# Six weight slots, 56 score blocks, small passes on GpSimd: a new plan for a fused attention and MLP kernel

## The chip, the cores and the metric

The kernel runs on one core of a Trainium2 chip. The metric is the device time of one execution in microseconds (us); the kernel before takes 736.29 us, the median of three runs that lie between 736.22 and 736.51. The engines are called as the profile calls them: PE is TensorE (matmul), PEld its weight loads, DVE is VectorE, ACT is ScalarE, POOL is GpSimd, SP is SyncE, which here only issues DMAs. PSUM has eight banks; a bank holds one block of 128 x 512 fp32.

## What is computed

```
x: 2048 x 512, 32 heads of 16                        # bf16 everywhere
g = sigmoid((x * gate_w).sum(-1))
q, k, v = split(x @ wqkv)
a = (softmax(q k^T / 4) v) @ wo                      # attention
h = gelu(layernorm(x) @ w1)                          # mixer MLP
x1 = x + shift(h) @ w2                               # four quarters, moved by 1, -1, 2, -2 rows
b = x1 + gelu(layernorm(x1) @ w3) @ w4               # w3: 512 x 1792, w4: 1792 x 512
out = g * a + (1 - g) * b
```

## The kernel before

**Scores.** There are 32 rounds (4 chunks of 512 queries, 4 groups of 8 heads, and the even or the odd heads of a group). A round has 64 score tiles: 16 blocks of 128 keys for each of 4 heads, which sit in four 32-row strips of PE. That makes 2048 tiles of 128 x 512. The q of a round is stored with the other four heads set to zero: that is what the two masks mE and mO do (L1209 to 1212). A QK matmul (L1482) writes a tile to a bank, and one of two engines turns it into exp(score). ACT takes two or three banks in one instruction (L1577). DVE instead makes bf16 bits by a linear map (L1609, "p1"), and then three more copies of the block with a constant added to the bits (L1652 on DVE, L1654 on POOL); the four together approximate the exponential. So a tile of ACT needs one PV matmul and a tile of DVE four (L1707). `close_pair` decides which of the three added copies of a pair go to DVE and which to POOL, by the numbers GP2 and GP3.

**Score blocks.** The exp values of a tile wait for their PV matmuls in one of NPROB = 40 blocks of `prob` (L887, L934). A pair of DVE tiles that has begun holds one of NTOK = 3 tokens until its last copy is made.

**The rest.** Projections, the MLP and the output projection are matmuls in column strips (`gen`, L1105 to 1131), each followed by an evacuation of its bank on DVE. Layernorm (`normalise`, L1290) makes rs on POOL and nm on DVE, then 32 passes over 128 x 512 on DVE (L1304); each result is written to DRAM (L1308) and read back transposed (L1314). The passes of L1366 multiply x1 by 1 - g. The three Gelu blocks run on ACT (L1324).

**Weights.** NW = 9 slots of 4 KB a partition hold the transposed x chunks, wk, wv, w1, w2, w3 and w4; each of w3 and w4 is loaded once. `wo` has a tile of its own (L901).

**The order.** Nothing is scheduled on the chip. A model of the engines in the kernel's own code (`Sim`) runs at build time: it takes jobs by priority, by when their inputs are ready and by free slots, and writes down the order of every queue, which the engines then follow with semaphores. Its choices are steered by some 30 numbers (`BASE`, L524) which `STEPS` (L548 to 881) changes every eight tiles. Other work enters by the count of score tiles done: `P_W1`, `P_W3`, `P_LD` and the like (L504 to 520). A POOL instruction and a DVE pass with `port=True` are never planned at once, and the POOL one gets a dependency on the last such DVE pass (`in_port_order`, L319).

**The start.** x chunk 0 comes by two plain DMAs, one from SP and one from the ACT queue (L1029), is transposed by 16 PE matmuls against an identity (L1143), copied out by ACT and DVE (L1155), and projected in column strips into kT and q (`k_first`, L1161; L1200, L1202). Chunks 2 and 3 are read by transposing DMAs (L1038), four each, all from SP.

**The end.** Behind the last PV matmul DVE forms the denominators of the last round (L2082 to 2085) and the last oT (L2092); PE adds the known part of the output (L2060), and four blocks are evacuated (L2099, L2101) and stored by four DMAs (L2103).

Of the kernel before, what the change touches and what calls it, by code (L numbers as in the profile page):

```python
# [470 lines left out]
def kernel(  # L471
# [48 lines left out]
    P_LD = (450, 888)  # L520
# [28 lines left out]
        0: dict(S_PRIO=0.3, GP2=1, DVE_STOP_L=7, SL0=0, IDLE_NS=864, BRES=2, AHEAD=16, AT_SH=69, HOLE=3, CAP3=5,  # L549
            AFIRST=1, AGE=20000),  # L550
        1: dict(DVE_STOP=2, URG=3, GATE=3, E_PRIO=0.1),
        2: dict(MAXU=4),
        3: dict(P1_PRIO=0.743, SL1=130, BRES=0, PV_IDLE=0.117, HOLE=2, RES=1),
        4: dict(P1_PRIO=0.414, GP2=0, DVE_STOP=6, URG=5, SL1=60, IDLE_NS=374, AHEAD2=24, PV_IDLE=0.731, MAXU=9, ROT=3,
            HOLE=7, MAXG=2, CAP3=0, RES=0, E_PRIO=2),
        5: dict(GP3=0.633, PV_FULL=0.947, LIMD=2, AGE=12000, JOIN=2),
        6: dict(URG=11, SL0=60),
        7: dict(GP2=0.655, GP3=0.967, DVE_STOP=13, URG=5, AHEAD2=13, PV_FULL=0.916, PRESS=15, MAXG=1, LIMD=3, AFIRST=0,
            AGE=20000, ROWM=3, LIMA=4, JOIN=0),
        8: dict(P1_PRIO=0.136, GP2=1, DVE_STOP=6, URG=2, DVE_ALONE=-81, SL0=0, B_LOW=5, AHEAD2=16, PRESS=18, MAXU=7,  # L560
            ROT=2, GATE=2, E_PRIO=0.25, AFIRST=1, ROWM=99, LIMA=3, JOIN=1),
# [12 lines left out]
        19: dict(SL0=130, AHEAD2=32, AFIRST=0),
        20: dict(S_PRIO=0.38, GP2=1, DVE_STOP=6, DVE_STOP_L=16, URG=5, EARLY=99, SL0=0, B_LOW=8, PV_FULL=0.813,
            PV_IDLE=0.117, PRESS=26, MAXU=7, ROT=3, AT_SH=69, HOLE=7, E_PRIO=0.25, AFIRST=1),
        21: dict(B_LOW=2, PRESS=22, MAXU=3, AT_SH=0, CAP2=5, LIMD=3),
        22: dict(URG=11, DVE_WAIT=4, DUE_SH=0),
        23: dict(URG=5, B_LOW=8, DVE_WAIT=3, PV_FULL=0.86, PRESS=26, DUE_SH=-14, AT_SH=69, CAP2=6, CAP3=4, LIMD=4),
        24: dict(IDLE_NS=459, AFIRST=2),  # L580
        25: dict(P1_PRIO=0.414, S_PRIO=0.178, DVE_STOP=13, IDLE_NS=864, B_LOW=5, AHEAD2=24, PV_FULL=0.97, PV_IDLE=0.731,
            PRESS=11, MAXU=2, ROT=0, DUE_SH=0, MAXG=3, AFIRST=1, ROWM=3),
        26: dict(S_PRIO=0.5),
        27: dict(S_PRIO=0.178, GP3=1, DVE_STOP=8, SL1=0, IDLE_NS=537, PV_FULL=1, PV_IDLE=0.117, PRESS=18, ROT=2,
            DUE_SH=16, MAXG=1, AFIRST=0),
# [417 lines left out]
    def W(name):  # L1003
        return wb[name].slot
# [1128 lines left out]
```

## Time and profile before

| | before |
|---|---|
| median of three runs | 736.29 us |
| the profiled execution | 735.27 us |
| its span, first to last instruction | 733.3 us |
| granted TensorE clock | 0.999 |
| busy: PE, DVE, ACT, POOL | 723.8, 698.6, 720.0, 452.7 us |
| DMA | 34.60 MB, mean 47 GB/s |

The profiled execution is the one from which all durations come; 2.0 us of its time lie outside the span. In a row of a group, the numbers behind the bar are the busy time of the group, the mean duration of one instruction in ns, and how long its engine stood idle just before such instructions, with what ended that. Two neighbours on an engine overlap in the trace, so the step from one start to the next is shorter than the duration. The ends of matmuls are modelled, so PE looks busy while it holds a finished result.

### The profile page before, as it was taken

The numbers are of one execution on the slowest core, as the hardware profiler recorded it, in microseconds if no ns is written. First come the engines' busy times: TensorE is split into PE (matmuls) and PEld (weight loads), VectorE is DVE, ScalarE is ACT, GpSimd is POOL, SyncE is SP. The second block draws the span as 40 slices with busy tenths as digits, with TensorE's granted clock in tenths as the row PEclk, the third lists the DMA queues.
The fourth block names the chain that finished last, engine by engine and source line by source line (L and its number), as shares of the span: only waits on it lengthen the run. The fifth ranks groups of instructions, "written<-read, shape, count | busy, mean of one in ns | idle before, by whom it ended". The sixth has DMA issues, their size and how long they took to land.

```text
span 733.3 us, 23826 instructions
## 1 busy us (share of the span) xinstructions
PE 723.8 (99%) x9517; PEld 212.3 (29%) x9518; DVE 698.6 (95%) x1493; ACT 720.0 (98%) x751; POOL 452.7 (62%) x452
## 2 busy tenths in 40 slices
PE   9999999999999999999999999999999999999997
PEld 5434322222222222222322222222222232222222
DVE  6999999999999999999999999999999999999997
ACT  7999999999999999999999999999999999999995
POOL 3456685778867666658545555566576765575442
PEclk9999999999999999999999999999999999999999
DMA  8504223111212033024100100001100010000001
GB/s 189 162 19 77 80 66 71 28 45 57 72 49 53 21 96 69 21 81 96 32 25 10 46 28 21 27 23 43 27 20 18 7 32 24 28 26 19 14 22 41
DMA packets 67094, 34.60 MB, mean 47 GB/s; under 512 B 46748, under 2 KB 62380, under 8 KB 66984
## 3 DMA queue, kind: packets, MB, share of 16 engines
q1 hardware_dynamic: 66040, 32.56, 17.7%
q8 instruction: 74, 1.21, 0.7%
q10 hardware_dynamic: 944, 0.52, 0.2%
q14 instruction: 36, 0.29, 0.2%
HBM read 17.40 MB, written 6.81 MB: 33 GB/s over the span
## 4 chain that ended last, share of the span: by engine, by line
PE 64%; ACT 11%; DVE 4%; issue 2%; POOL 0%; ACTq 0%; DVEq 0%
PE banks L1707 24%; PE banks L1482 22%; PE banks L1112 17%; ACT prob L1577 6%; ACT hT L1324 2%; ACT hB L1324 2%; DVE prob L1609 1%; DVE prob L1652 1%; ACT L1324 1%; DVE x_sb L1357 0%; ACT L1326 0%; DVE st L1284 0%; DVE w L1415 0%; POOL prob L1654 0%; PE banks L2060 0%
## 5 line engine op out<-in xcount | busy, mean ns | idle before, releaser
L1577 ACT ACTIVATE prob<-banks 128x1024 bf16<-128x1024 f32 (+1 forms) x728 | 675.5, 1102 | 1.1 <-PE banks L1482 0.2
L1654 POOL TENSOR_SCALAR prob<-prob 128x1024 uint16<-128x1024 uint16 x390 | 400.3, 1045 | 233.4 <-DVE prob L1652 110.9
L1609 DVE TENSOR_SCALAR prob<-banks 128x512 uint16<-128x512 f32 x577 | 380.3, 684 | 17.4 <-PE banks L1482 12.9
L1707 PE MATMUL banks<-prob,V 128*17 128x512 bf16 (+1 forms) x3785 | 321.6, 381 | 0.2
L1482 PE MATMUL banks<-q,kT 32*128 32x512 bf16 x2048 | 280.1, 384 | 1.5 <-ACT prob L1577 0.7
L1652 DVE TENSOR_SCALAR prob<-prob 128x1024 uint16<-128x1024 uint16 x480 | 179.5, 422 | 2.0 <-PE banks L1707 0.6
L1482 PEld LDWEIGHTS <-kT 32*128 32x128 bf16 x2048 | 70.0, 90 | 295.3 <-ACT prob L1577 269.2
L1707 PEld LDWEIGHTS <-V 128*17 128x17 bf16 (+1 forms) x3785 | 71.8, 88 | 116.7 <-issue 94.9
L1112 PE MATMUL banks<-xnT,w 128*32 128x512 bf16 x1152 | 89.4, 383 | 0.0
L1112 PE MATMUL banks<-w,hT 128*32 128x512 bf16 x688 | 64.5, 384 | 0.0
L1746 POOL TENSOR_TENSOR oT<-accsb,bcs 128x512 bf16<-128x512 f32 x31 | 39.5, 1273 | 26.7 <-DVE prob L1652 21.5
L1112 PEld LDWEIGHTS <-w 128*32 128x32 bf16 x1936 | 41.0, 95 | 48.9 <-issue 27.0
L1112 PE MATMUL banks<-w,w 128*32 128x256 bf16 (+1 forms) x784 | 41.5, 308 | 0.4 <-DVE prob L1609 0.4
L1112 PE MATMUL banks<-w,hB 128*32 128x512 bf16 x448 | 36.0, 382 | 0.6 <-ACT hB L1324 0.6
L1123 PE MATMUL banks<-wo,oD 32*128 32x512 bf16 x64 | 24.6, 384 | 0.0
L1112 PEld LDWEIGHTS <-hT 128*32 128x32 bf16 x688 | 15.9, 95 | 20.5 <-issue 15.1
L1284 DVE BATCH_NORM_STATS2 st<-x_sb 128x6 f32<-128x512 bf16 x32 | 21.5, 678 | 0.0
L1728 DVE COPY accsb<-banks 128x512 f32<-128x512 f32 x31 | 21.1, 680 | 0.2 <-PE banks L1707 0.2
L1112 PE MATMUL banks<-wo,oD 128*32 128x512 bf16 x176 | 21.0, 384 | 0.0
L1112 PE MATMUL banks<-w,wq 128*32 128x512 bf16 x256 | 19.4, 382 | 1.0 <-DVE accsb L1728 1.0
L1378 DVE CAST hB<-banks 128x512 bf16<-128x512 f32 x28 | 19.0, 682 | 0.9 <-PE banks L1112 0.9
L1324 ACT ACTIVATE hT<-hT 128x7168 bf16<-128x7168 bf16 (+1 forms) x3 | 19.4, 6452 | 0.0
(94 smaller groups left out, 246.8 us busy)
## 6 DMA issues: line engine op xcount, KB each, us to landing
bcs<-rr SPq DMA_DIRECT2D x124, 64.0 KB
xn_dram<-xn SPq DMA_DIRECT2D x32, 128.0 KB
w<-in_B_w_dram SPq DMA_DIRECT2D x5, 512.0 KB
oD<-oT SPq DMA_DIRECT2D x124, 16.0 KB
w<-in_B_w_dram SPq DMA_DIRECT2D x4, 448.0 KB
out_dram<-ot SPq DMA_DIRECT2D x14, 128.0 KB
x_sb<-in_A_x_dram SPq DMA_DIRECT2D x3, 512.0 KB
w<-in_A_wqkv_dram SPq DMA_DIRECT2D x2, 256.0 KB
```

What stands on the lines that cost most here:

```text
L1112: units.append([Op("col", j, lambda j=j, lf=lf, rf=rf, n0=n0, n1=n1, st=st, sp=sp: nc.tensor.matmul(get()[32 * j:32 * j + 32, n0:n1], lhsT ...
L1123: o = Op("row", i, lambda: nc.tensor.matmul(get(), lhsT=lf(0, P)[rows], rhs=rf()[rows], start=False, stop=True, tile_position=(32 * i, 0), ...
L1284: a = dve(600, deps, lambda: nc.vector.bn_stats(out=sb.slot[:], in_=x_sb[:, t, :]), prio=6, at=at, acq=[sb])
L1324: g = nc.scalar.activation(out=ap, in_=ap, func=ACT.Gelu_apprx_tanh)
L1482: o = Op("row", i, lambda: nc.tensor.matmul(dst(), lhsT=kT[G][32 * i:32 * i + 32, kt * P:(kt + 1) * P], rhs=qbuf[G, c].slot[32 * i:32 * i ...
L1577: job = act(hold, ops, lambda: nc.scalar.activation(out=prob[:, pb.cut(), :].bitcast(BF16), in_=unit()[:, rb.cut(), :], func=ACT.Exp, scal ...
L1609: return nc.vector.tensor_scalar(out=prob[:, b0.cut() if w == 2 else b0.bufs[h0].slot, :], in0=unit()[:, rb.cut() if w == 2 else rb.bufs[0 ...
L1652: return nc.vector.tensor_scalar(out=cut(k), in0=cut(0), scalar1=float(SHIFT * k), scalar2=None, op0=ALU.add)
L1654: return nc.gpsimd.tensor_scalar(out=cut(k), in0=cut(0 if both else 2), scalar1=1.0, scalar2=float(SHIFT * (k if both else 1)), op0=ALU.mu ...
L1707: return nc.tensor.matmul(one(accs[r])[32 * i:32 * i + n, :], lhsT=lhs(n), rhs=rhs(), start=st and not edge, stop=True, tile_position=(0, ...
L1728: e = dve(PSUM_NS, round_ops[r], lambda: nc.vector.tensor_copy(out=ab.slot[:], in_=one(accs[r])), acq=[ab], prio=0, frees=[accs[r], Call(a ...
L1746: n = gp(1250, d3, lambda: nc.gpsimd.tensor_tensor(out=ob.slot[:], in0=ab.slot[:], in1=bb.slot[:], op=ALU.mult), acq=[ob], frees=[ab, bb], ...
```

## The change

1. NPROB goes from 40 to 56, NTOK from 3 to 5, NW from 9 to 6. `wo` moves into one of the six slots. w3 and w4 are loaded twice, once for each pair of chunks, so eight more loads are issued; w2 and wo are loaded later (tile 330 and 855). The windows of w1 and of the second half of w3 begin later.
2. 76 passes of 128 x 512 go from DVE to POOL: 30 masks of q, 32 of layernorm, 14 products with 1 - g.
3. Chunk 0 of x is no longer loaded and transposed by PE: four transposing DMAs read it, slices 0 and 2 from SP, 1 and 3 from ACT. Twelve full-array matmuls (`first`) make q and kT of it; ACT and DVE evacuate half of q each. x_sb of chunk 0 is loaded later, for the layernorm alone.
4. At the end the first two output blocks leave in one DMA, all known parts come behind the last PV, and y of the last chunk lies in the slots of `xnT`.
5. A few durations in the model change, and `STEPS` is replaced throughout.

```diff
-    P_W1 = (143, 440)
+    P_W1 = (195, 445)
-    P_W3 = ((610, 710), (710, 840), (1200, 1390), (1400, 1570))
+    P_W3 = ((610, 710), (710, 840), (1245, 1400), (1410, 1570))
-    P_LD = (450, 888)
+    P_LD = ((450, 1190), (845, 1575))
...
-    NPROB, NTOK, NW = 40, 3, 9
+    NPROB, NTOK, NW = 56, 5, 6
...
-    xa, xb = (start(e, 3000.0, lambda q, a=a: q.dma_start(out=x_sb[:, a:a + 2, :], in_=x_src(0, a, a + 2)))
-              for e, a in (("SP", 0), ("ACT", 2)))
+    def xT_dma(c, part, k):
+        return lambda q: q.dma_start(out=W(f"x{c}{part}")[:, k, :], in_=x_by_d[c * 512:(c + 1) * 512, k], transpose=True)
     dl_w["q0"] = start("SP", 2600.0, col(wq, 0, 128))
     dl_w["k0"] = start("ACT", 2900.0, col(W("k"), D, D + 128))
+    for k in range(KT):
+        j_xT[0, 0, k] = start(("SP", "ACT")[k % 2], 2000.0, xT_dma(0, 0, k), 1800.0 if k < 2 else 1300.0)
+    j_x1 = [start("SP", 2600.0, lambda q: q.dma_start(out=x_sb[:, 4:8, :], in_=x_src(1, 0, 4)))]
...
+    def first(t):
+        qb = qbuf[0, 0] = Buf("q", 128)
+        bq, ba, bb = (Buf("bank", 1) for _ in range(3))
...
+        def mm():
+            for k in range(KT):
+                for b, w, n0, n1 in ((bq, wq, 0, 512), (ba, W("k"), 0, 256), (bb, W("k"), 256, 512)):
+                    guard(b, nc.tensor.matmul(one(b)[:, 0:n1 - n0], lhsT=w[:, k, 0:P], rhs=W("x00")[:, k, n0:n1], start=k == 0,
+                                              stop=k == KT - 1, skip_group_check=True))
+        def evacuate():
+            nc.scalar.activation(out=qb.slot[:, 0, 0:256], in_=one(bq)[:, 0:256], func=ACT.Copy, scale=mE[:])
+            nc.vector.tensor_scalar(out=qb.slot[:, 0, 256:512], in0=one(bq)[:, 256:512], scalar1=mE[:], scalar2=None,
+                                    op0=ALU.mult)
+            sim.readers[ba] = [nc.scalar.copy(out=kT[0][:, 0:256], in_=one(ba)[:, 0:256])]
...
         for p, m in ((0, mE), (1, mO)):
-            j_q[G, c, p] = dve(262, [e, j_m3] + ([j_q[G, c, 0]] if p else []), lambda p=p, m=m: nc.vector.tensor_scalar(
-                out=qb.slot[:, p, :], in0=qf.slot[:], scalar1=m[:], scalar2=None, op0=ALU.mult), prio=0.3, port=True,
+            j_q[G, c, p] = gp(600, [e, j_m3] + ([j_q[G, c, 0]] if p else []), lambda p=p, m=m: nc.gpsimd.tensor_scalar(
+                out=qb.slot[:, p, :], in0=qf.slot[:], scalar1=m[:], scalar2=0.0, op0=ALU.mult, op1=ALU.add), prio=0.3,
...
-            g = dve(323, [m], lambda t=t, xb=xb: nc.vector.tensor_scalar(
+            g = gp(600, [m], lambda t=t, xb=xb: nc.gpsimd.tensor_scalar(
                 out=xb.slot[:], in0=x_sb[:, t, :], scalar1=rs[which][:, t:t + 1], scalar2=nm[which][:, t:t + 1],
...
-            jx1g[t] = dve(262, [last[t % 4], jgate], lambda t=t: nc.vector.tensor_scalar(
+            jx1g[t] = gp(600, [last[t % 4], jgate], lambda t=t: nc.gpsimd.tensor_scalar(
...
-                    ybuf[tt // 2] = Buf("w", 10 ** 6)
+                    ybuf[tt // 2] = Buf("xnT", 10 ** 6)
...
-    for k in range(KT):
-        x_transposes(0, (k,), j_x0)
-    k_first()
-    q_proj(0, 0, -1)
+    first(6200.0)
...
-    for cs in PAIRS:
+    for cs, at3, at4 in zip(PAIRS, *P_LD):
+        for i in range(KT):
+            wload(f"3{i}", B_w3[i * P:(i + 1) * P, :], 2 * FT)
+            dl_w[f"3{i}"].prio, dl_w[f"3{i}"].at = 6, at3 + 10 * i
+        for i in range(4):
+            wload(f"4{i}", B_w4[512 * i:min(F, 512 * (i + 1)), :], 8)
+            dl_w[f"4{i}"].prio, dl_w[f"4{i}"].at = 7, at4 + 10 * i
         mlp2(cs, s2, at_of, gate_job)
...
     for tt in (1, 3):
-        add_y(tt, tt not in early)
-    for tt in range(4):
-        if tt not in early:
-            known(tt, range(LG, 4), tt % 2 == 0)
+        into(tt, idf[:], y_of(tt), True)
+        known(tt, False)
+        known(tt - 1, True)
...
+        if tt == 1:
+            nc.sync.dma_start(out=out_flat[(t - 1) * P:(t + 1) * P, :].rearrange("(t p) d -> p t d", p=P), in_=both[:, 0:2, :])
+        elif tt > 1:
+            (nc.scalar if tt == 3 else nc.sync).dma_start(out=out_flat[t * P:(t + 1) * P, :], in_=o)
```

More of the change, by code (lines that the diff above doesn't have):

```diff
@@ L1068 @@
     wload("2", B_w2, 16)
[L1069 to L1070 removed]
+    dl_w["2"].at = 330
+    wload("o", A_wo, 10 ** 6)
+    dl_w["o"].at = 855
     def ident():
@@ L1390, in mlp2_down @@
     def mlp2_down(c, ge, bb, h2, jx1g, at_of):
+        w4 = [wb[f"4{i}"] for i in range(4)]
         for t in range(4 * c, 4 * c + 4):
```

763 lines of the change are left out of this document (353 added, 410 removed).

## The prediction

> **What bounds the kernel now.** I read the page first: the span, the busy time of each engine, and the costliest groups.
>
> ```profile
> span 733.3 us, 23826 instructions
> PE 723.8 (99%) x9517; PEld 212.3 (29%) x9518; DVE 698.6 (95%) x1493; ACT 720.0 (98%) x751; POOL 452.7 (62%) x452
> ...
> L1577 ACT ACTIVATE prob<-banks 128x1024 bf16<-128x1024 f32 (+1 forms) x728 | 675.5, 1102 | 1.1 <-PE banks L1482 0.2
> L1654 POOL TENSOR_SCALAR prob<-prob 128x1024 uint16<-128x1024 uint16 x390 | 400.3, 1045 | 233.4 <-DVE prob L1652 110.9
> L1609 DVE TENSOR_SCALAR prob<-banks 128x512 uint16<-128x512 f32 x577 | 380.3, 684 | 17.4 <-PE banks L1482 12.9
> ...
> L1652 DVE TENSOR_SCALAR prob<-prob 128x1024 uint16<-128x1024 uint16 x480 | 179.5, 422 | 2.0 <-PE banks L1707 0.6
> ```
>
> Three engines look full, and ACT is: 728 exponentials with 1.1 us of idle time before them in all. The view by windows gives the same by stage (the columns after the stretch and its length are PE, PEld, DVE, ACT and POOL, then granted clock, DMA share and GB/s). The first row runs from the first exponential to the end of the last.
>
> ```profile
> 8.50:724.70 716.20, 712.43 (x9423) 206.50 (x9423) 692.21 (x1478) 715.01 (x743) 448.84 (x438) 1.00 0.18 45
> ...
> 80.00:360.00 280.00, 278.92 (x3535) 78.90 (x3529) 270.22 (x572) 279.73 (x285) 199.63 (x197) 1.00 0.23 59
> 360.00:720.00 360.00, 358.09 (x4645) 97.25 (x4638) 348.98 (x734) 359.65 (x380) 210.89 (x202) 1.00 0.09 24
> ```
>
> ACT works 715.0 of 716.2 us. So the end is set by when ACT begins, how many tiles it gets, and the 8.6 us behind its last one. PE is no bound of its own, which the list of waits shows:
>
> ```profile
> PEld L1482 <- ACT prob L1577: 269.2, 645, 0.8
> POOL prob L1654 <- DVE prob L1652: 110.9, 85, 4.4
> ...
> DVE prob L1609 <- PE banks L1482: 12.9, 45, 0.8
> ```
>
> The weight loads of the score matmuls stand 269 us until ACT frees a bank. ACT can only be relieved by giving tiles to DVE, which is busy 692 of the same 716 us. The second row hides a fourth resource. POOL idles 280 us, but 110.9 us of it, 85 times, until a DVE copy ends. The timeline shows what happens there:
>
> ```profile
> 202.15 2.05 POOL L1654 TENSOR_SCALAR prob<-prob 128x1024 uint16<-128x1024 uint16 x2
> ...
> 204.43 0.37 DVE L1652 TENSOR_SCALAR prob<-prob 128x1024 uint16<-128x1024 uint16 x1
> ...
> 205.13 0.73 DVE L1304 TENSOR_SCALAR xn<-x_sb,rs,nm 128x512 bf16<-128x512 bf16 x2
> ...
> 205.94 0.47 POOL L1293 TENSOR_SCALAR rs<-mv 128x4 f32<-128x4 f32 x2 [1.75 <-DVE xn L1304]
> ```
>
> POOL ends at 204.20, stands 1.75 us while DVE makes copies and layernorm passes from SBUF to SBUF, and starts when they end. POOL and these DVE passes take turns, as `in_port_order` writes it. The turn is well used: POOL 452.7 + copies 179.5 + the passes to be moved 26.7 (below) = 659 of 733 us. In 80 to 360 us it is 199.63 of POOL and
>
> ```profile
> 80.00:360.00 280.00, 54.58 (x149) 1.00 0.23 59
> ```
>
> of L1652 alone, 254 of 280 us (91%) before the passes to be moved are counted.
>
> **The 76 passes.** The rows by form:
>
> ```profile
> L1577 ACT ACTIVATE prob<-banks 128x1024 bf16<-128x1024 f32 x715 | 659.7, 1095 | 0.8 <-PE banks L1482 0.2 <-DVE prob L1652 0.2 <-ACT prob L1577 0.2
> ...
> L1577 ACT ACTIVATE prob<-banks 128x1536 bf16<-128x1536 f32 x13 | 19.3, 1487 | 0.2
> ...
> L1304 DVE TENSOR_SCALAR xn<-x_sb,rs,nm 128x512 bf16<-128x512 bf16 x32 | 12.1, 404 | 1.1 <-DMA xn_dram<-xn 1.1
> ...
> L1210 DVE TENSOR_SCALAR q<-qf,mO 128x512 bf16<-128x512 bf16 x15 | 5.3, 350 | 0.0
> L1210 DVE TENSOR_SCALAR q<-qf,mE 128x512 bf16<-128x512 bf16 x15 | 5.1, 342 | 0.0
> ...
> L1366 DVE TENSOR_SCALAR x_sb<-x_sb,omg 128x512 bf16<-128x512 bf16 x14 | 4.2, 344 | 0.0
> ```
>
> DVE loses 12.1 + 5.3 + 5.1 + 4.2 = 26.7 us. On POOL a pass of 512 isn't shown: its bounds are half of L1654's 1.045 and the whole, 0.52 and 1.05 us. I take 0.6, half plus a little that doesn't shrink: 76 x 0.6 = 45.6 us. The turn thus grows by 45.6 - 26.7 = 18.9 us.
>
> What the freed DVE time buys follows from four prices. ACT has 715 x 2 + 13 x 3 = 1469 of the 2048 tiles, DVE 579. A tile that goes over saves ACT 675.5 / 1469 = 0.460 us. It costs DVE (380.3 + 179.5) / 579 = 0.967 and the turn (179.5 + 400.3) / 579 = 1.001. A copy of a pair that goes back from POOL to DVE costs DVE 179.5 / 480 = 0.374 and frees 400.3 / 390 - 0.374 = 0.652 of the turn. Let x tiles and y copies move, let all idle times stay, and let the three shrink alike by g: 0.460 x = g; 26.7 - 0.967 x - 0.374 y = g; 0.652 y - 18.9 - 1.001 x = g. That gives g = 3.2 us, with x = 7 and y = 45. Without copies going back the turn would be overfull in the stretch above, where layernorm lies; that end is rival two. Three more PV matmuls for each of 7 tiles lie in PE's 269 us.
>
> **56 blocks, five tokens.** At best all 17.4 us of idle time before p1 go; put into the second equation that is 3.5 us more. At worst nothing. I take nothing, since 12.9 of the 17.4 end with a score matmul, and not with a block that comes free. For the middle: -3.2, between -6.7 and, by rival two, +8.
>
> **Reloaded weights.** Eight more issues on SP and 3.6 MB at nothing: behind 360 us the DMA engines are 9% busy (the third row of the windows), and w3 and w4 are wanted by PE, which has slack. If that cover goes (a slot not yet free, and the loads of the softmax denominators queued behind it on SP), the MLP slips by some us inside a window of 100 tiles, still off ACT's path. Likewise POOL's copies wait behind a layernorm pass that waits for nm; 110.9 us of POOL idle time cover it. The longer model times for Gelu run nowhere.
>
> **The start.** The rows, from the first loads to the first exponential, and two pairs of DMAs in which the second waits for the first:
>
> ```profile
> 0.74 0.46 SPq L1029 DMA_DIRECT2D x_sb<-in_A_x_dram  x1
> ...
> 1.25 0.46 SPq L1027 DMA_DIRECT2D wq<-in_A_wqkv_dram  x1
> ...
> 2.85 6.02 SPq L1038 DMA_TRANSPOSE w<-in_A_x_dram  x4
> ...
> 4.62 1.45 PE L1143 MATMUL banks<-idb,x_sb 128*128 128x128 bf16 x16
> ...
> 8.05 0.37 ACT L1169 CAST kT<-banks 128x256 bf16<-128x256 f32 x1 [0.19 <-PE banks L1112]
> ...
> 8.10 0.60 PE L1482 MATMUL banks<-q,kT 32*128 32x512 bf16 x5
> 8.54 4.62 ACT L1577 ACTIVATE prob<-banks 128x1536 bf16<-128x1536 f32 x4
> ```
>
> ```profile
> 38.35 0.64 SPq L1730 DMA_DIRECT2D den<-accsb  x1
> 40.13 0.36 SPq L1732 DMA_DIRECT2D pk<-den  x1
> ...
> 216.60 0.90 SPq L1308 DMA_DIRECT2D xn_dram<-xn  x2
> 220.00 2.48 SPq L1314 DMA_TRANSPOSE xnT<-xn_dram  x2
> ```
>
> From the last slice of x to the first exponential there will be the last three matmuls (0.6), half of q and half of kT on ACT (0.37 each, the row at 8.05), and from QK to exp 0.44 (8.10 to 8.54): 1.8 us. When the last slice lands is the open point, since before has all its transposing DMAs on one queue. **Side by side:** SP issues slices 0 and 2 from 1.25, a step of 6.02 / 4 = 1.5, ACT likewise; the last begins at 2.75 and lands 2.95 (217.05 to 220.00, 128 KB) to 3.9 us (0.74 to 4.62) later. First exponential at 7.5 to 8.5, a gain of 1.0 to 0. **Chained,** each waiting for the one before on the other queue to land: 1.25 + 4 x 1.78 (the small DMA, 38.35 to 40.13) to 1.25 + 3.9 + 3 x 2.95, first exponential at 10.2 to 15.8, a loss of 1.6 to 7.3. In the middle, 1.25 + 3.0 + 3 x 2.5 = 11.75, so 13.55: a loss of 5.0.
>
> I take the chained case at 5.0, with 2.5 a step because the 128 KB row is nearer than the small one. [...] ACT can't begin its own table load before its two DMAs are out, and what SP loads next waits too. [...]
>
> **The end.**
>
> ```profile
> 725.41 1.98 PE L2060 MATMUL banks<-w,idf 128*128 128x512 f32 x4
> ...
> 727.23 0.59 PE L2060 MATMUL banks<-wo,oD 128*128 128x512 bf16 x2
> ...
> 728.06 1.04 PE L2060 MATMUL banks<-woL,oT 128*128 128x512 bf16 x4 [0.24 <-DVE oT L2092]
> ...
> 729.16 0.74 DVE L2101 SCALAR_TENSOR_TENSOR xn<-banks,omg,w 128x512 bf16<-128x512 f32 x1
> ...
> 730.20 0.40 SPq L2103 DMA_DIRECT2D out_dram<-xn  x1
> ```
>
> Two more known parts come behind the last PV, 0.2 us each, so 727.82 becomes 728.2 where the last oT is ready at 728.06: 0.2 lost. The third store waited from 729.90 to 730.20 behind two issues, of which one goes: 0.3 won. Nothing in sum.
>
> **The sum.** Against the profiled execution's own 735.27 us: + 5.0 for the start, - 3.2 for the passes, 0 for the rest, 737.1. The median of the runs, 736.29, stands 1.0 above the profiled execution, so the forecast is 738.1 us, 0.2% slower and a little more; 0.2%, about 1.5 us, is what a measurement of this kernel can tell from no change.
>
> **The rivals.**
>
> One, on the other side: the four transposing DMAs run side by side. For it: on one queue the next transposing DMA begins 1.5 us behind the last without waiting for it to land, and both queues feed the same DMA engines. [...] Then 735.27 - 0.5 - 3.2 + 1.0 = 732.6. It decides as soon as the last slice lands before 8.54 - 1.8 = 6.7 us.
>
> Two: the turn becomes the bound. For it: 91% of the turn is taken between 80 and 360 us before the moved passes, and 32 layernorm passes and 14 products lie between w1 and w3, thus in that stretch. 46 x 0.6 = 27.6 us of POOL for 46 x 0.38 = 17.5 us of DVE add 10 us to a turn that then has no more than that free, and a mask or a copy that comes late holds blocks and tiles. Against it: 1.75 us of POOL idle time at a layernorm are the order's doing and can be planned away, and copies can go back to DVE. It decides where POOL and the DVE passes together reach the length of the stretch. With the start chained, up to 8 us lost in the middle in place of 3.2 won; at half of that, 735.27 + 5.0 + 4.0 + 1.0 = 745.3.
>
> Three: blocks and tokens do all that they could, 3.5 us more. For it: 5 tokens let five pairs be under way while POOL is at layernorm. Against it: what ends DVE's idle time is a score matmul. 738.1 - 3.5 = 734.6.
>
> **How the numbers follow.** The forecast 0.42, rival one 0.25, two 0.20, three 0.13. The forecast's own range, the step of the chain and the price of a POOL pass within their bounds, is 735 to 742. The range is 730 to 747: down to rival one with two or three us more from blocks, up to rival two at a little over half of its 8 us. Faster by over 0.2% is below 734.8: nearly all of one, over half of three, 0.31. Slower is above 737.8: four fifths of the forecast and all of two, 0.54. Between lies 0.15.
>
> **What would show it.** The start: the transposing DMAs of the ACT queue begin only when one of SP has landed, the fourth at about 9 us, and the first exponential starts near 13.5 us; side by side it starts before 8.6. The middle: ACT has 7 to 15 exponential tiles fewer, DVE as many more; DVE copies rise by some 45 and POOL's fall; the moved passes last about 0.6 us. Rival two: waits of POOL on DVE copies give way to DVE standing idle ahead of L1652's line, and ACT no longer at 99% between 80 and 360 us. Blocks: idle time before p1 falls well below 17.4 us. The prediction fails if the start is not later, if ACT's tiles change by far more than 7 (an order that packs DVE differently from the old one, which no row of before can show), or if stalls appear at the second load of w3, between 430 and 460 us.

## The result, and the profile after

The changed kernel takes 742.63 us (median of 4 runs, 742.40 to 742.96) against 736.27 of the kernel before: 1.0086 times, 95% interval [1.0069, 1.0103]. It is slower, as forecast, and lies 4.5 us above the forecast of 738.1 and inside the range of 730 to 747. The profiled execution took 742.96 (before: 735.27), its span 741.0. First the page of the changed kernel: the span, the engines, and the costliest groups (busy us and mean ns of one, then idle us before them and what ended it).

```profile
span 741.0 us, 23758 instructions
...
PE 726.2 (98%) x9536; PEld 215.5 (29%) x9537; DVE 699.6 (94%) x1447; ACT 715.6 (97%) x732; POOL 483.8 (65%) x504
...
L1560 ACT ACTIVATE prob<-banks 128x1024 bf16<-128x1024 f32 (+1 forms) x710 | 672.3, 1105 | 5.6 <-PE banks L1465 4.3
L1637 POOL TENSOR_SCALAR prob<-prob 128x1024 uint16<-128x1024 uint16 x366 | 376.2, 1046 | 196.0 <-DVE prob L1635 115.8
L1592 DVE TENSOR_SCALAR prob<-banks 128x512 uint16<-128x512 f32 (+1 forms) x576 | 381.7, 689 | 12.0 <-PE banks L1465 8.1
...
L1635 DVE TENSOR_SCALAR prob<-prob 128x1024 uint16<-128x1024 uint16 x513 | 197.6, 436 | 2.3 <-PE banks L1690 0.6
```

The plan did what the forecast's middle term supposed for ACT: 668 x 2 + 42 x 3 = 1462 tiles (the rows by form below) in place of 1469, seven fewer. DVE made 33 copies more (513 for 480), where 45 were forecast. But ACT's idle time before exponentials grew from 1.1 to 5.6 us.

```profile
L1560 ACT ACTIVATE prob<-banks 128x1024 bf16<-128x1024 f32 x668 | 621.2, 1080 | 2.6 <-PE banks L1465 2.0 <-DVE prob L1635 0.2
L1560 ACT ACTIVATE prob<-banks 128x1536 bf16<-128x1536 f32 x42 | 63.1, 1503 | 3.0 <-PE banks L1465 2.3 <-PE banks L1086 0.4
```

The view by windows (busy time of PE, PEld, DVE, ACT, POOL, then granted clock, DMA share, GB/s); the first row runs from the first exponential to the end of the last:

```profile
15.60:732.47 716.87, 713.26 (x9490) 210.25 (x9490) 693.15 (x1433) 711.83 (x725) 479.88 (x490) 1.00 0.20 51
...
360.00:720.00 360.00, 359.60 (x4664) 97.66 (x4665) 352.76 (x729) 359.95 (x379) 224.35 (x221) 1.00 0.13 34
```

Call the time from the start of the first exponential to the end of the last the stretch of exponentials. Against the same row of before: the first exponential starts 7.1 us later (15.60 for 8.54), ACT works 3.2 us less (711.83 for 715.01), and yet the stretch is 0.8 us longer (716.87 for 716.11), because ACT idles in it for 5.0 us and not 1.1. Nearly half of that idle time, 2.3 us, lies in its first 40 us; before has 0.02 there. Behind the last exponential lie 8.53 us for 8.65. The sum of the three, 7.06 + 0.76 - 0.12, is what the span gained, 7.7. From 360 us on ACT is busy 359.95 of 360, and from 430 to 460, where the prediction looked for stalls at the second load of w3, 30.00 of 30: the reloaded weights, whose transfers lie there, cost nothing.

The timeline of the start (start, length, engine, line, operation; in brackets the idle time before it and what ended it):

```profile
1.25 1.28 ACTq L1002 DMA_TRANSPOSE w<-in_A_x_dram  x1
...
4.54 1.23 SPq L1002 DMA_TRANSPOSE w<-in_A_x_dram  x1
...
7.19 1.14 ACTq L1002 DMA_TRANSPOSE w<-in_A_x_dram  x1
7.21 0.58 PE L1148 MATMUL banks<-w,wq 128*128 128x512 bf16 x1 [1.75 <-DMA w<-in_A_x_dram]
...
7.60 0.63 PE L1148 MATMUL banks<-w,w 128*128 128x256 bf16 x2
...
9.79 1.13 SPq L1002 DMA_TRANSPOSE w<-in_A_x_dram  x1
10.96 0.58 SPq L1008 DMA_DIRECT2D x_sb<-in_A_x_dram  x1
...
12.43 0.58 PE L1148 MATMUL banks<-w,wq 128*128 128x512 bf16 x1 [3.35 <-DMA w<-in_A_x_dram]
...
12.81 0.63 PE L1148 MATMUL banks<-w,w 128*128 128x256 bf16 x2
...
13.24 0.63 PE L1148 MATMUL banks<-w,wq 128*128 128x512 bf16 x1
...
13.66 0.63 PE L1148 MATMUL banks<-w,w 128*128 128x256 bf16 x2
...
14.53 0.39 ACT L1164 CAST kT<-banks 128x256 bf16<-128x256 f32 x1
...
14.95 1.01 PE L1465 MATMUL banks<-q,kT 32*128 32x512 bf16 x5 [0.66 <-ACT kT L1164]
...
15.60 2.37 ACT L1560 ACTIVATE prob<-banks 128x1536 bf16<-128x1536 f32 x2 [0.69 <-PE banks L1465]
```

The transposes are chained: ACT, SP, ACT, SP, each 2.6 to 3.3 us after the one before. The list of waits says the same of SP's queue: its transposes stood 7.3 us, in two waits, until a transfer of x had landed. That is the case on which the forecast was built. Three things in these rows were not in it. Matmuls start 0.38 to 0.43 us apart, twice as far as in e2 below (0.21 to 0.24), and they do so behind the wait of 3.35 us and ahead of it (7.21, 7.60). The last of three evacuations on ACT, at 14.53, is what the first scores wait for; the forecast counted two. And the load of the second chunk of x leaves SP at 10.96, where before it left at 1.75.

### The profile page after: what moved, and what is told of

Its sections match the earlier page's. It is cut to its first block, busy times and chain, and to the rows that moved or that the text cites. A ratio compares the mean times of both kernels' runs of the same rounds, so it can differ in the third digit from the quotient of the medians.

```text
span 741.0 us, 23758 instructions
## 1 busy us (share of the span) xinstructions
PE 726.2 (98%) x9536; PEld 215.5 (29%) x9537; DVE 699.6 (94%) x1447; ACT 715.6 (97%) x732; POOL 483.8 (65%) x504
## 4 chain that ended last, share of the span: by engine, by line
PE 58%; ACT 2%; DVE 2%; issue 1%; DVEq 0%; ACTq 0%
PE banks L1690 23%; PE banks L1465 20%; PE banks L1086 15%; ACT hB L1307 1%; DVE prob L1592 1%; DVE prob L1635 1%; PE banks L2040 0%; ACT prob L1560 0%; ACT hT L1307 0%; ACT L1309 0%; ACT L1307 0%; DVE accsb L2051 0%; DVE accsb L1711 0%; ACT w L2068 0%; DVE qf L1191 0%
## 5 line engine op out<-in xcount | busy, mean ns | idle before, releaser
L1637 POOL TENSOR_SCALAR prob<-prob 128x1024 uint16<-128x1024 uint16 x366 | 376.2, 1046 | 196.0 <-DVE prob L1635 115.8
L1592 DVE TENSOR_SCALAR prob<-banks 128x512 uint16<-128x512 f32 (+1 forms) x576 | 381.7, 689 | 12.0 <-PE banks L1465 8.1
L1690 PE MATMUL banks<-prob,V 128*17 128x512 bf16 (+1 forms) x3806 | 317.6, 381 | 1.0 <-POOL prob L1637 0.4
L1635 DVE TENSOR_SCALAR prob<-prob 128x1024 uint16<-128x1024 uint16 x513 | 197.6, 436 | 2.3 <-PE banks L1690 0.6
L1086 PE MATMUL banks<-xnT,w 128*32 128x512 bf16 x1152 | 93.4, 383 | 0.1
L1086 PE MATMUL banks<-w,hT 128*32 128x512 bf16 x696 | 60.7, 384 | 0.0
L1086 PEld LDWEIGHTS <-w 128*32 128x32 bf16 x1904 | 40.7, 96 | 51.7 <-issue 29.2
L1287 POOL TENSOR_SCALAR xn<-x_sb,rs,nm 128x512 bf16<-128x512 bf16 x32 | 24.7, 776 | 8.7 <-DVE prob L1635 5.5
L1097 PE MATMUL banks<-w,oD 32*128 32x512 bf16 x64 | 24.2, 384 | 0.0
L1360 DVE CAST hB<-banks 128x512 bf16<-128x512 f32 x28 | 18.9, 676 | 0.0
L1360 DVE CAST hT<-banks 128x512 bf16<-128x512 f32 x28 | 18.9, 675 | 0.0
```

What stands on the lines that cost most here:

```text
L1086: units.append([Op("col", j, lambda j=j, lf=lf, rf=rf, n0=n0, n1=n1, st=st, sp=sp: nc.tensor.matmul(get()[32 * j:32 * j + 32, n0:n1], lhsT ...
L1097: o = Op("row", i, lambda: nc.tensor.matmul(get(), lhsT=lf(0, P)[rows], rhs=rf()[rows], start=False, stop=True, tile_position=(32 * i, 0), ...
L1287: g = gp(600, [m], lambda t=t, xb=xb: nc.gpsimd.tensor_scalar(out=xb.slot[:], in0=x_sb[:, t, :], scalar1=rs[which][:, t:t + 1], scalar2=nm ...
L1360: pre.append(evac(g, PSUM_NS, lambda ps, m=m: nc.vector.tensor_copy(out=h2()[:, m, :], in_=ps[:])))
L1592: return nc.vector.tensor_scalar(out=prob[:, b0.cut() if w == 2 else b0.bufs[h0].slot, :], in0=unit()[:, rb.cut() if w == 2 else rb.bufs[0 ...
L1635: return nc.vector.tensor_scalar(out=cut(k), in0=cut(0), scalar1=float(SHIFT * k), scalar2=None, op0=ALU.add)
```

## The experiments

Times are compared as ratios to the kernel before on the same chip, with 95% intervals; 0.001 is 0.74 us. The theory at the outset: the start costs the whole loss, and the rest (passes, blocks, order) gains one to three us. The rivals: the moved passes fill the turn of POOL and DVE and cost time; or one of the parts at the start, and not the chain, makes it dear.

### e1: all four transposes from SP's queue

```diff
-start(("SP", "ACT")[k % 2], 2000.0, xT_dma(0, 0, k), ...)
+start(("SP", "ACT")[k % 2], 2000.0, lambda q, k=k: xT_dma(0, 0, k)(nc.sync), ...)
```

> The changed kernel, every queue in the same order, but all four transposing DMAs of chunk 0 issued from SP. Theory (the start is a chain over two queues): from one queue they follow each other every 1.3 us from 1.25 us on, the last lands near 8 us, the first exponential starts near 10 us and not at 15.6, and chunk 1 of x is asked for near 6.5 us and not at 10.96. Time 742.6 - 5.8 for the start - about 2 for tiles that no longer come late = 735, 733 to 738. Rival (DMA landing is slow whatever the queue): first exponential still at 14 us or later, time above 740.

Measured: 1.0023 [1.0006, 1.0040], a median of 737.05 (expected 733 to 738), though two of the eleven executions took 739.78 and 742.70. The profiled span is 734.4, the first exponential starts at 9.71, the stretch of exponentials is 716.15. Its timeline:

```profile
1.25 5.15 SPq L1002 DMA_TRANSPOSE w<-in_A_x_dram  x4
...
7.81 0.38 PE L1148 MATMUL banks<-w,wq 128*128 128x512 bf16 x1 [0.43 <-DMA w<-in_A_x_dram]
```

From one queue the four follow each other in 1.3 us, without waiting for each other, and the last has landed by 7.81 in place of 12.43. Of the change's 0.0086, 0.0063 is the two-queue chain with all that follows from it (the later loads, and the pace of PE, which in e1 doubles at about 6.6 us: matmuls start 0.42 us apart at 6.11 and 0.22 at 6.79). The time comes from the hand-over between queues (2.6 to 3.3 us a step for 1.3) and not from the transposes.

### e2 and e2_again: the changed order with the start on TensorE

```diff
+nc.sync.dma_start(out=x_sb[:, 0:2, :], in_=x_src(0, 0, 2))
+nc.scalar.dma_start(out=x_sb[:, 2:4, :], in_=x_src(0, 2, 4))
...
-    j_xT[0, 0, k] = start(..., xT_dma(0, 0, k), ...)
+    j_xT[0, 0, k] = start(..., lambda q: None, ...)
...
+            for k in range(KT):
+                for s in range(4):
+                    nc.tensor.transpose(out=half(k)[:, s * P:(s + 1) * P], in_=x_sb[:, s, k * P:(k + 1) * P], identity=idb[:])
+            for k in range(KT):
+                (nc.vector.tensor_copy if k % 2 else nc.scalar.copy)(out=W("x00")[:, k, :], in_=half(k))
```

> The changed kernel with the start of before: x chunk 0 by two plain DMAs, transposed by PE, copied by ACT and DVE; chunk 1 asked for at 1.75 us as before. The rest of every queue keeps the new order. Theory (the new order with its passes, blocks and reloads is itself faster, and all of the loss is the start): first exponential near 8.5 us, 7.1 us earlier, and the 10 to 12 tiles that the changed kernel lacks after its first 80 us come back, some 3.5 us: 742.6 - 7.1 - 3.5 = 732, 730.5 to 734, below before's 736.3. Rival (the new order or the passes on POOL cost time as well): only the 7.1 us come back or less, 735.5 to 739.

> The kernel of e2 once more, beside the three, to see whether its 0.9986 [0.9977, 0.9995] repeats: 0.997 to 1.000 if the new order is worth the 1.3 us that its stretch of exponentials showed; 1.000 to 1.001 if it is not, as f1 (1.0 [0.9991, 1.0009]) would have it.

Measured: 0.9986 [0.9977, 0.9995], a median of 734.65 that lies just above the expected 730.5 to 734, and a second time 0.9993 [0.9984, 1.0002]. With a start like that of before, the loss is gone. The second run's stretch of exponentials, and rows of its timeline:

```profile
9.10:723.62 714.52, 711.79 (x9490) 208.96 (x9490) 694.88 (x1434) 711.57 (x725) 480.84 (x490) 1.00 0.20 50
```

```profile
4.59 1.06 PE L1153 MATMUL banks<-idb,x_sb 128*128 128x128 bf16 x16
...
9.10 5.05 ACT L1570 ACTIVATE prob<-banks 128x1536 bf16<-128x1536 f32 x4 [0.47 <-PE banks L1475]
...
9.18 1.07 PE L1119 MATMUL banks<-idb,x_sb 128*128 128x128 bf16 x16
```

The stretch is 714.52 (714.80 in the first run), 1.3 to 1.6 us shorter than before. ACT's work falls by 3.4 us (711.57 for 715.01) and its idle time rises from 1.1 to 2.95 (3.4 in the first run). Passes, blocks and new order together are thus worth 1.3 to 1.6 us, and about 0.5 us of that goes to a first exponential that is later than before's 8.54. The whole is at the edge of what can be measured: faster once, not to be told from before the second time.

### e3: the chained start in the kernel before

```diff
-xa, xb = (start(e, 3000.0, lambda q, a=a: q.dma_start(out=x_sb[:, a:a + 2, :], in_=x_src(0, a, a + 2)))
-          for e, a in (("SP", 0), ("ACT", 2)))
+xa, xb = (start(e, 3000.0, lambda q: None) for e in ("SP", "ACT"))
...
+for k in range(KT):
+    (nc.sync, nc.scalar)[k % 2].dma_start(out=W("x00")[:, k, :], in_=x_by_d[0:512, k], transpose=True)
```

> The kernel before, in its own order, with one part of the change alone: chunk 0 by four transposing DMAs, slices 0 and 2 from SP, 1 and 3 from ACT, no PE transposes and no copies out of PSUM for it, x_sb of chunk 0 loaded later. Theory (chain, and what SP loads behind it comes late): first exponential near 15.5 us, and early tiles late by some 3 us more: 736.3 + 7 + 3 = 746, 743.5 to 748. Rival (the later loads hide): 736.3 + 7.0 = 743.3 or less.

Measured: 1.0182 [1.0158, 1.0206]. The rows of its first slice-bound matmuls and of its first exponential:

```profile
12.41 1.05 PE L1115 MATMUL banks<-w,wq 128*32 128x512 bf16 x8 [4.52 <-DMA w<-in_A_x_dram]
...
15.54 2.37 ACT L1582 ACTIVATE prob<-banks 128x1536 bf16<-128x1536 f32 x2
```

The chain lands at 12.41 here too and the first exponential is 7.0 us late. But the loss is 13 us by the ratio and 15 in the profiled execution, more than expected, since the stretch of exponentials grows from 716.1 to 724.5: the order was made for data that come earlier, and behind the start ACT idles 7.4 us in its first 40. From 30 to 40 us PE is busy only 5.24 of the 10, and its granted clock falls to a half once more, from 35.6 to 42.4 (a mean of 0.78 from 30 to 40 us and of 0.94 from 40 to 60). Eighty us after the first exponential 199 tiles are done where before had 222, and 640 us after it the deficit is still 26. In this fixed order the late start wasn't regained. The changed kernel, whose order expects the transposing DMAs, loses less; that its planning is the reason is argued, not shown.

### e4: the passes on POOL in the kernel before

```diff
-dve(262, ..., nc.vector.tensor_scalar(out=qb.slot[:, p, :], ..., scalar2=None, op0=ALU.mult)
+dve(262, ..., nc.gpsimd.tensor_scalar(out=qb.slot[:, p, :], ..., scalar2=0.0, op0=ALU.mult, op1=ALU.add)
```

and the same for xn and x_sb; the order is that of before.

> The kernel before, with another part alone: the 76 passes run on POOL, each at the place in the order that it had on DVE; nothing is planned anew, so ACT and DVE keep their tiles. Theory (ACT sets the end, the turn has room): DVE loses 26.7 us of work and idles more, the time stays, 736.3 within 1.5 us. Rival two of the prediction (the turn is full between 80 and 360 us): POOL copies come late there, PV and with it blocks and banks, and the time grows by 3 to 8 us, 739 to 744.

Measured: 1.0124 [1.0109, 1.0140]. The windows and the layernorm pass on POOL:

```profile
200.00:300.00 100.00, 96.70 (x1190) 27.14 (x1188) 87.92 (x164) 94.44 (x102) 91.37 (x99) 0.98 0.21 53
```

```profile
L1304 POOL TENSOR_SCALAR xn<-x_sb,rs,nm 128x512 bf16<-128x512 bf16 x32 | 29.6, 931 | 9.5 <-DVE prob L1652 3.3 <-issue 3.1 <-DMA xn_dram<-xn 1.9
```

This is rival two's mechanism, in rival two's place: between 200 and 300 us POOL is busy 91.37 of 100 us, for 68.89 before, DVE falls from 96.85 to 87.92 and ACT from 99.84 to 94.44. The whole costs 9 us (rival two: 8), a little above the 739 to 744 that were expected for it. In the changed kernel it does not occur: in the same stretch POOL is busy 79.51, DVE 97.74 and ACT 99.11. That the plan gave 33 copies back to DVE is the likely reason; no run takes them away alone.

### f1 and f2: an earlier start, and the passes back on DVE

f1 is e2 with its first evacuations spread over two engines (the transposed slices also lie in other banks):

```diff
-for k in range(KT):
-    for b, w, n0, n1 in ((bq, wq, 0, 512), (ba, W("k"), 0, 256), (bb, W("k"), 256, 512)):
+for b, w, n0, n1 in ((bq, wq, 0, 512), (ba, W("k"), 0, 256), (bb, W("k"), 256, 512)):
+    for k in range(KT):
...
-sim.readers[ba] = [nc.scalar.copy(out=kT[0][:, 0:256], ...)]
+sim.readers[ba] = [nc.vector.tensor_copy(out=kT[0][:, 0:256], ...)]
```

> The changed kernel's order with the start on TensorE as in e2, its steps rearranged: the two evacuating engines read different banks, the four q matmuls come before the eight of kT, and kT's first half is evacuated by VectorE while ScalarE works on q. In e2 the first exponential was held by three evacuations in a row on ScalarE (7.61 to 8.62). If the start is a plain loss that runs through to the end: q done at 5.87 + 4 x 0.21 = 6.7, both halves of q by 7.2, kT done at 7.6, last half evacuated by 8.0, first exponential at 8.4 (e2: 9.085), time 734.65 - 0.65 = 734.0, 0.9976 of the kernel before. Rival: another delivery (the value weights, chunk 1) sets the pace behind the start, and the idle time of ScalarE grows by what the start gained: 734.6, no change against e2.

f2 is f1 with the 76 passes executed by DVE at the places planned for POOL:

```diff
-gp(600, ..., lambda t=t, xb=xb: nc.gpsimd.tensor_scalar(out=xb.slot[:], ...)
+gp(600, ..., lambda t=t, xb=xb: nc.vector.tensor_scalar(out=xb.slot[:], ...)
```

and the same for q and x_sb.

> f1 with the 76 small passes executed by VectorE at the places where the order had planned them for GpSimd; nothing planned anew. This is the mirror of e4. If moving the passes is worth something in this order: VectorE takes on 76 passes of 0.29 to 0.38, 26 us more, against about 20 us of idle time in the whole span of which 12 lie ahead of the score passes, and ScalarE runs out of banks: 740 to 748. Rival (GpSimd's 0.73 us for a pass under the turn costs VectorE as much as the passes themselves did, so that the move is neutral): the turn falls by 76 x 0.4 = 30 us and the time stays within 2 us of f1.

Measured: f1 1.0000 [0.9991, 1.0009], no gain (a median of 735.32 for the expected 734.0); f2 1.0119 [1.0105, 1.0133]. In f1's profiled execution the first exponential starts at 9.77. PE's sixteen transposes begin there as early as in e2_again, and without a wait among them, but take 1.91 us for 1.06:

```profile
4.61 1.91 PE L1153 MATMUL banks<-idb,x_sb 128*128 128x128 bf16 x16
```

f1's PE reaches its full pace only at about 7.0 us (q matmuls start 0.33 us apart at 6.78, 0.22 behind 7.11), e2_again's at 4.6, when its sixteen begin. f2, with the same start, is busy 3.3 us with its eleven matmuls on zeros, where before takes 3.7, and has its first exponential at 8.83. So this start depends on when PE's pace doubles, which differed between these executions, and f1's profile does not test what the rearranged steps are worth; the expected 8.4 was not reached. f2's stretch of exponentials:

```profile
8.83:732.31 723.48, 716.53 (x9490) 210.81 (x9490) 708.21 (x1510) 715.38 (x725) 425.36 (x414) 1.00 0.20 49
```

DVE takes on 13 us net (708.21 for e2_again's 694.88) and the stretch grows by 9. The median, 744.15, falls into the expected 740 to 748, and it is the mirror of e4: moving the passes alone costs 1.2% in either direction. Neither run shows a price of the move apart from the order: each order fits the engine that it was planned for.

### f3 and f4: planned anew with one number changed

```diff
-NPROB, NTOK, NW = 56, 5, 6
+NPROB, NTOK, NW = 40, 3, 6
```

> f1 with 40 score blocks and 3 tokens, as the kernel before has them, planned anew with the changed kernel's own settings. If the blocks are worth nothing (the forecast): the same time as f1 but for the scatter between two plans, which f4 shows; 733 to 737, ScalarE's idle time between 2 and 5 us. Rival three of the prediction (the blocks bring what there is): 737 or more, with ScalarE idle at places where all 40 blocks are held, above 6 us in all. The settings were chosen for a plan with 56 blocks, so a slower time alone would not settle it.

```diff
-j_q[G, c, p] = gp(600, ...
+j_q[G, c, p] = gp(690, ...
...
-g = gp(600, [m], ...
+g = gp(760, [m], ...
-jx1g[t] = gp(600, ...
+jx1g[t] = gp(690, ...
```

> f1 with the planner told what the passes were measured to cost on GpSimd (0.69 for q and the residual rows, 0.76 for the normalised rows, in place of 0.60) and planned anew, all else alike. If the mis-priced passes cost the order something: ScalarE idle below 2 us, VectorE taking a few copies more, 733 to 734. If they cost nothing, this shows the scatter between two plans: 733 to 737.

Measured: f3 1.0612 [1.0598, 1.0627], f4 1.0687 [1.0671, 1.0704]. Both expectations were wrong by 40 us and more. ACT's row in f4:

```profile
L1570 ACT ACTIVATE prob<-banks 128x1024 bf16<-128x1024 f32 (+1 forms) x714 | 680.1, 1122 | 45.8 <-PE banks L1475 26.9 <-POOL xn L1297 7.2 <-PE banks L1700 6.9
```

A correction of 0.09 to 0.16 us in the planner's price of 76 passes, with `STEPS` left as it was, makes ACT idle 45.8 us before exponentials. Two plans scatter by far more than anything this study wants to see. So f3 says nothing on the blocks, and what 56 blocks and five tokens are worth stays open. What remains is that DVE's idle time before p1 fell from 17.4 to 12.0 us in the changed kernel.

### g1, g2, g3: what the start costs behind the chain

g1 uses the slices in the order in which they land (the marks of the first and the last matmul of a bank move along):

```diff
-for k in range(KT):
+for k in (1, 0, 3, 2):
```

> The changed kernel with the twelve matmuls of its first projections in the order in which the slices land (second, first, fourth, third) in place of numeric order; nothing else. In the changed kernel the third slice lands last (12.43) and two slices' worth of matmuls, six, run behind it. If the order of use is part of what the forecast missed: three matmuls behind 12.43 in place of six, first exponential 15.60 - 0.85 = 14.75, time 742.63 - 0.85 = 741.8, 1.0075 of the kernel before. Rival (the fourth slice is not there earlier than the third, because the queue that issues it waits): no change, 15.6.

g2 also lets PE multiply zeros while it waits:

```diff
+    for _ in range(12 if k == 3 else 0):
+        nc.tensor.matmul(banks_of((NBANK - 1,))[:, NBANK - 1, 0:384], lhsT=zero[:, 0:P], rhs=zero[:], ...)
...
-for _ in range(13):
+for _ in range(18):
```

> g1 with matmuls on zeros that keep TensorE busy while it waits for slices: 18 in place of 13 ahead of the first slice, 12 between the second and the third. If the double duration of the matmuls behind the wait (steps of 0.38 to 0.43 where they take 0.21 in e2, the first scores 1.01 where they took 0.60) comes from TensorE having stood still: the three matmuls take 0.45 in place of 0.85, the first scores 0.6 in place of 1.0, first exponential 14.75 - 0.8 = 13.95, time 741.0. Rival (the duration comes from the transposes' traffic into memory, which goes on): no change against g1.

g3 is the changed kernel with two loads ahead of SP's transposes:

```diff
 dl_w["q0"] = start("SP", 2600.0, col(wq, 0, 128))
+nc.sync.dma_start(out=x_sb[:, 4:8, :], in_=x_src(1, 0, 4))
+col(W("v"), 2 * D, 2 * D + 256)(nc.sync)
```

> The changed kernel with the loads of the second chunk of x and of the first value weights issued by SP ahead of its transposes, so that they no longer wait behind the chain (10.96 and 11.59 in the changed kernel). Nothing else. If the 2.07 us that the stretch of exponentials is longer than in e2 (716.87 against 714.80) come from these late loads: the stretch 714.8 to 715.3, ScalarE idle some 2 us in place of 4.0, the chain not longer, time 742.63 - 1.8 = 740.8. Rival (768 KB beside the chain slow every transpose): first exponential at 16.5 to 18, time unchanged or up to 744.

Measured in the profiles: first exponential at 14.52 in g1 (expected 14.75), at 13.74 in g2 (13.95), at 14.91 in g3. g1's timeline, then its windows of PE alone (busy, granted clock, DMA share, GB/s):

```profile
12.20 0.59 PE L1148 MATMUL banks<-w,wq 128*128 128x512 bf16 x1 [1.59 <-DMA w<-in_A_x_dram]
...
12.58 0.63 PE L1148 MATMUL banks<-w,w 128*128 128x256 bf16 x2
```

```profile
8.00:9.00 1.00, 0.00 (x0) 1.00 0.54 125
...
10.00:13.00 3.00, 1.41 (x6) 0.50 0.44 76
...
19.00:19.50 0.50, 0.50 (x11) 0.50 0.82 272
...
20.00:20.50 0.50, 0.50 (x16) 1.00 1.05 347
```

PE, which waits for slices, is granted half its clock from about 9.7 us on and gets it back at about 19.9 us, long after the start. g2's timeline and windows:

```profile
11.85 0.38 PE L1151 MATMUL banks<-w,wq 128*128 128x512 bf16 x1 [1.43 <-DMA w<-in_A_x_dram]
...
12.06 0.38 PE L1151 MATMUL banks<-w,w 128*128 128x256 bf16 x2
...
13.31 0.59 PE L1468 MATMUL banks<-q,kT 32*128 32x512 bf16 x5 [0.86 <-ACT kT L1167]
...
13.74 2.37 ACT L1563 ACTIVATE prob<-banks 128x1536 bf16<-128x1536 f32 x2 [0.47 <-PE banks L1468]
...
14.96 1.89 PE L1117 MATMUL banks<-idb,x_sb 128*128 128x128 bf16 x16 [1.07 <-DMA x_sb<-in_A_x_dram]
```

```profile
10.00:13.00 3.00, 1.01 (x6) 1.00 0.40 68
...
14.00:14.50 0.50, 0.00 (x0) 0.50 1.10 354
```

Kept busy, PE starts its matmuls 0.21 us apart, the first scores take 0.59 in place of 1.01, and the first exponential is 0.78 us earlier than in g1; 0.8 was expected. The doubled duration thus comes from PE having had too little work (busy 0.39 us from 8 to 10 us in g1, 2.00 in g2) and not from the transfers (76 GB/s from 10 to 13 us in g1, 68 in g2). But then PE waits 1.07 us for the late second chunk of x, the clock halves at 14.0, the 16 transposes take 1.89 in place of 1.07, and the stretch of exponentials is 717.16. By time, g1 with 1.0092 [1.0078, 1.0106] and g2 with 1.0085 [1.0071, 1.0098] can't be told from the changed kernel's 1.0086: the 1.1 and 1.9 us that the first exponential won are not shown to reach the end, and in g2 0.5 of it went into a longer stretch (717.16 for g1's 716.62), with the next wait. The expected 741.8 and 741.0, 1.0075 and 1.0064 of the kernel before, were too hopeful, though the mechanism holds.

g3, timeline and stretch:

```profile
14.91 5.05 ACT L1562 ACTIVATE prob<-banks 128x1536 bf16<-128x1536 f32 x4 [0.47 <-PE banks L1467]
...
14.99 1.07 PE L1119 MATMUL banks<-idb,x_sb 128*128 128x128 bf16 x16
```

```profile
14.91:729.29 714.38, 711.43 (x9490) 209.43 (x9490) 694.14 (x1434) 711.48 (x725) 480.68 (x490) 1.00 0.20 51
```

g3 takes 1.0076 [1.0061, 1.0092], a median of 740.30 where 740.8 was expected; by the ratio it can't be told from the changed kernel either. Its profiled span is 737.8. Its stretch of 714.38 is that of e2_again (714.52), as expected: the 2 us that the changed kernel lost behind its first exponential are gone in this profile. It is not only the loads, though. In g3 both of ACT's slices leave before both of SP's, so there is one hand-over and not three, and PE gets its slices so late and close together that it works without a break from 10.33 until the last slice is used, and has its full pace before the first scores (five of them take 0.59 us, 1.01 in the changed kernel). Late loads and half clock together are the 2 us. Each can do it. In the changed kernel the second chunk of x was there when PE came to it, in g1 PE waited 0.24 us for it, and still ACT idles 1.9 and 1.8 us in the first 20 us of the stretch: there the half clock is what the traces show (0.50 in g1, score matmuls of 603 ns in the changed kernel). In e1 PE has its full pace from 6.6 us on and only the loads are late (PE waits 0.87 us for the second chunk), and its stretch is 1.6 us longer than e2_again's all the same. How the two divide in the changed kernel was not settled.

## Why the prediction was right, and where it was off

The direction and the mechanism of the loss were right, the size was not, and part of the hit is luck. The forecast's own range, 735 to 742, ends below the measured 742.63; it lies in the full range because of the part above 742, which was there for rival two, and rival two did not come.

**The start** was the step that failed in size. The mechanism was right: chained, across two queues, by the wait that the forecast named. The step was 2.65, 2.60 and 2.64 us for a forecast 2.5, the first 3.29 for 3.0, so the last slice landed at 12.43 for 11.75. The larger miss lay behind it: 3.17 us from there to the first exponential for 1.8. Six matmuls stood behind the last slice and not three, because the third slice lands last and is used before the fourth, and PE ran at half its pace (matmuls 0.38 to 0.43 us apart): 1.47 us to the first evacuation for 0.6. ACT made three evacuations in a row and not two, which took 1.05 us for 0.74; the second half of kT is on ACT too, and the sum left it out. From QK to exp it took 0.65 for 0.44, again at half the pace (five score matmuls in 1.01 us for 0.60). Together 7.1 us of loss for 5.0, inside the bounds of 1.6 to 7.3.

**What SP loads next** was named ("what SP loads next waits too") and given no price. With the half clock it cost 2 us of ACT's idle time (5.0 in the stretch for 2.9 in g3 and e2_again). This is the term that was missing from the sum.

**The middle**, -3.2, was right for ACT's work (7 tiles, 3.2 us less) and too good for the stretch: with the start of e2 it gives -1.3 to -1.6, as ACT idles 1.8 to 2.3 us more. The price of a POOL pass, 0.6, was too low. In the changed kernel:

```profile
L1287 POOL TENSOR_SCALAR xn<-x_sb,rs,nm 128x512 bf16<-128x512 bf16 x32 | 24.7, 776 | 8.7 <-DVE prob L1635 5.5 <-issue 1.7 <-POOL xn L1287 1.0
L1193 POOL TENSOR_SCALAR q<-qf,mO 128x512 bf16<-128x512 bf16 x15 | 10.8, 721 | 5.4 <-DVE prob L1635 4.2 <-DVE V L1213 1.2
L1193 POOL TENSOR_SCALAR q<-qf,mE 128x512 bf16<-128x512 bf16 x15 | 10.4, 692 | 4.2 <-DVE prob L1635 4.2
L1349 POOL TENSOR_SCALAR x_sb<-x_sb,omg 128x512 bf16<-128x512 bf16 x14 | 10.0, 719 | 5.7 <-DVE prob L1635 5.6
```

That is 55.9 us for 76 passes, 0.74 each, so the turn grows by 29.2 and not 18.9; put into the prediction's three equations it gives 2.0 in place of 3.2. That this is why ACT idles more is argued, not shown.

**Reloads and end** cost nothing, as forecast. **Blocks** stay open.

**The rivals.** One (side by side) did not happen. For a start at which the transposes need no wait between queues, e1 shows a first exponential at 9.71, even so 1.2 us later than before, so rival one's gain of 0.5 was out of reach with one queue. Two's mechanism is real (e4) but did not come in the planned order, as the text against it said. Its condition was met, though: from 80 to 360 us POOL's 212.78 and the 66.12 of DVE's copies make 278.9 of 280 us, and still ACT idles only 1.2 us there. In e4 the same sum is 300.5, more than the stretch is long, so the durations of the two overlap in the trace, and neither rival two's condition nor the prediction's third equation is the strict limit that it was taken for. (Rival two's 17.5 us for 46 passes on DVE are 12.1 + 4.2 = 16.3 by the rows.) Three is not borne out: nothing near 3.5 us more came.

**The wait between the queues.** That each transposing DMA waits until the one before on the other queue has landed was an assumption of the author; no row of before shows such a wait, and the 5.0 us in the sum rest on it. The changed kernel shows it: each issue on the other queue stands 2.6 to 3.3 us behind the one before, while on one queue they follow in 1.3 us (e1), and the first exponential came 7.1 us later. What the wait is for was not shown.

## What to carry to other kernels

Keep transposing DMAs that are close in time on one queue: alternating two queues paid 2.6 to 3.3 us at every change of queue here, where one queue took 1.3 us a transpose, and everything later on both queues waited behind it. When the data of a start come late, count what PE does afterwards at a lower clock (here matmuls 0.38 to 0.43 us apart for 0.21), and what is queued behind the wait, not the wait alone. Before comparing two starts by one profile each, compare when PE reached its full pace in them. In a kernel whose order is planned with hand-set numbers, isolate a part by executing the same order differently, since a plan made anew with one number changed moved the time by 6 to 7%.

## What the runs showed of the hardware

In views of narrow windows PE's granted clock goes from 1.00 to 0.50 at 9.66 us in g1 and at 13.97 in g2, and is back at 1.00 at 19.90 and 20.80, 10.24 and 6.83 us later. In e3 it is 0.50 from 10 to 14 us, 1.00 again at about 15.1, and halved once more from 35.6 to 42.4. These times are worked out from the mean clock of the window in which a change lies (0.66 from 9.5 to 10 us in g1), with one change to a window. The next table has PE's busy time in stretches around the changes. (The ends of matmuls are modelled, so the busy times are rough.)

| run | stretch, us | PE busy, us | the clock |
|---|---|---|---|
| g1 | 6 to 9.5 | 0.91 | 1.00, falls to 0.50 at 9.66 |
| g2 | 10 to 13.5 | 1.20 | 1.00, falls to 0.50 at 13.97 |
| g1 | 10 to 13 | 1.41 | 0.50 |
| g1 | 14 to 16 | 1.75 | 0.50 |
| g1 | 16 to 20 | 4.00 | 0.50, back at 1.00 at 19.90 |
| g2 | 16 to 20 | 4.00 | 0.50, back at 1.00 at 20.80 |
| e3 | 12 to 16 | 3.59 | 0.50, back at 1.00 at about 15.1 |

The longest wait of PE ahead of the fall was 1.87 us in g1 and 1.43 in g2. The return followed no single length of work: until it came, PE had worked without a break for 2.7 us in e3 (from 12.41), 4.8 in g1 (from 15.12) and 5.8 in g2 (from 14.96). What sets the moments of these changes was not shown.

The pace changes at the start too. PE's first matmuls, on zeros, begin at 1.12 us in the timelines of before, the changed kernel, e1, e2 and g1 to g3, some 0.32 us apart, and the pace doubles at 4.6 us in e2_again, 6.6 in e1 and 7.0 in f1. In the changed kernel PE ran out of work at 5.46, before that had happened, and the pace doubles only at about 20.4 (three score matmuls are busy 0.61 us from 19.44 on and 0.39 from 21.24 on).

The granted clock of a profile can miss this. The views count a stretch as full clock until the first record of the clock in the trace, which in the changed kernel stands at 20.37 us. So its rows show 1.00 throughout the start, yet its score matmuls mean 603 ns from 15.5 to 21 us and 384 ns from 21.2 to 31:

```profile
L1465 PE MATMUL banks<-q,kT 32*128 32x512 bf16 x12 | 2.2, 603 | 0.7 <-ACT kT L1164 0.7
```

```profile
L1465 PE MATMUL banks<-q,kT 32*128 32x512 bf16 x28 | 3.5, 384 | 0.0
```

The duration of the same matmul form is the safer witness.
